# A planned attention and MLP kernel: the plan's charge for transposing DMAs, 0.8 to 0.67 and 0.5

## The chip, the cores and the metric

The kernel runs on one core of a Trainium2 chip, in one launch. The metric is the device time in microseconds (us) of that launch; of several runs the median is given. One execution more is taken with the hardware profiler. Its page and its trace count from the first to the last instruction, the span, and its own time is somewhat longer than its span.

The engines are TensorE (PE: matrix products; PEld: its weight loads), VectorE (DVE), ScalarE (ACT), GpSimd (POOL) and SyncE (SP). SyncE issues nearly all transfers; they run on 16 DMA engines that all transfers share.

## What is computed

A gated linear attention with a state per head, and behind it an MLP with a squared ReLU. The reference, cut to the arithmetic:

```python
# batch B=4, heads H=8, sequence S=768, head size D=48
for t in range(S):
    state = alpha[:, :, t, :, None] * state + np.einsum('bhd,bhe->bhde', k[:, :, t], v[:, :, t])
    y[:, :, t] = np.einsum('bhd,bhde->bhe', q[:, :, t], state)
x = y.transpose(0, 2, 1, 3).reshape(B * S, H * D)      # 3072 tokens x 384
h = x @ w_in                                           # 384 x 2048
r = np.maximum(h, 0.0)
out = (r * r) @ w_out                                  # 2048 x 384
```

Inputs and the output are float32; the products on TensorE are in bfloat16 with float32 sums.

## The kernel before

**Tiles.** The 3072 tokens are 24 chunks of 128, six to a batch entry. The attention works chunk by chunk: logarithms of alpha on ScalarE (L497), their running sums by a matmul with a triangle of ones (L530 to L546), exponentials of the sums (A, and their inverse) on ScalarE, and products of q with A and of k with the inverse on VectorE. Scores of a chunk are then a product of k and q (`e_p2`, L452), masked on VectorE (`sm`, L463, L472 and L473); the output is scores times v (L707) plus q times the state (L701). The state is updated by a matmul of k's product and v (L679), scaled on VectorE (L690), and copied to bfloat16 on ScalarE (L695).

Chunks 10 to 23 go in pairs (`DUO` = 10, `RAW` = 10): q and k are turned by a transposing DMA *before* they meet the exponentials. A q pair is loaded at L413, cast on GpSimd (L417) and turned by one transposing DMA (L420, tile rawt); k is loaded at L402, cast (L514) and a pair is turned by another (L517, tile aiT). VectorE multiplies the turned tiles with the exponentials (L610 for q, L613 for k). From chunk 18 on (`KTURN`) the k product is turned back by a transposing DMA for the state update (`e_kn`, L615). The casts of v (L506) are on GpSimd too.

The attention output is copied by ScalarE to `xn` (L487) and has to be turned once more, to be the MLP's moving operand `xT_big`. For chunks 14 to 22 (`XTURN`) a transposing DMA does it (`e_xt`, L729), for the others TensorE (L726) and a copy on VectorE (L489).

The MLP takes the chunks in groups, of two for the most part. Its first product with `w_in` goes to PSUM; ScalarE writes the ReLU `r` (L789), VectorE squares it into `gT` (L797); the second product takes `gT` and `w_out`; a copy on ScalarE or VectorE (L869, L871) moves the result out, and SyncE, or GpSimd for some, stores it. The first 16 chunks' outputs are held back (`keep`) and stored late, from L876.

**What sets the order.** No loop sets it. Each step is added to a plan as an operation with an engine, a duration in us, the operations that it depends on, and a latency. The plan then simulates the engines: at each step it starts the operation that can start first, and at equal times the one with the lower `prio`. In the end it sorts all operations by planned start and emits them in that order; each engine's queue gets its instructions in the order of emission and works them off in that order. A planned duration sets an order, then, and no time.

Loads are operations of a first-in-first-out engine called DMA (0.98 to 1.0 for 192 KB, 1.6 for a q pair). Transposing DMAs are of an engine called TR; each also keeps the engine DMA for its duration, in `Plan.run`, so that loads planned behind it start later:

```python
            if eng in ("OUT", "TR"):
                free["DMA"] = max(free.get("DMA", 0.0), t) + op.dur
            op.done = t + op.dur + op.lat
```

`TLD` is the charge for half a turned q or k pair (L420 and L517 are charged `2 * TLD`) and for the turned k product (L615 is charged `TLD`). `e_xt` has a charge of its own. `TLAT` and `XLAT` are the latencies behind the charges, `TLATE` and `late` put the instruction itself later in SyncE's queue than its planned start, so that loads can go ahead of it. A square of 128x512 on VectorE (L797) is charged 0.06 + 512/1850 = 0.34, a product of L610 or L613 0.34.

Which attention steps may run early is bounded by a gate: a chunk's sums may be added only when the MLP has come far enough. The instruction streams are the outcome of all of these together.

## Time and profile before

| what | before |
|---|---|
| median of 3 runs | 181.31 us (180.39 to 181.83) |
| the profiled execution | 181.09 us |
| its span | 179.4 us |
| granted TensorE clock, mean | 0.998 |
| HBM read, written | 25.17 MB, 4.72 MB |
| transposing DMAs xT, rawt, L615, aiT | 9, 7, 5, 7 |

The runs spread over 1.44 us, 0.8% of their median. The profiled execution is one run: its terms are added against its own 181.09, which is 1.7 above its span and 0.22 below the median.

Of a row in a timeline the first two numbers are start and length, then come engine, line, operation, what is written and read, and how many instructions were merged; square brackets tell of idle time before it. Rows of a DMA queue ("SPq") show the issue, not the transfer. Matmuls overlap each other: for two that follow each other the distance of their starts tells what one costs.

### The profile page before, as it was taken

To read this page: it belongs to the slowest core of one execution; us is meant where nothing else is said; L and a number is where in the kernel's file an instruction comes from. 1 tells how busy PE (TensorE), PEld (TensorE's weight loads), DVE (VectorE), ACT (ScalarE), POOL (GpSimd) and SP (SyncE) were. 2 spreads that over 40 slices of the span, in tenths; PEclk is the share of its full clock that TensorE was granted. 3 is DMA by queue.
4 is the path that set the end of the run, shared out by engine and by line. 5 is a ranking of instruction groups with operands and counts; after the bars stand their busy time and mean duration, and the time that the engine had idled before them with its cause. 6 is when DMAs were issued, how large, how long until landed. Compare 5 with 4: busy or idle time off the path is not lost.

```text
span 179.4 us, 4829 instructions
## 1 busy us (share of the span) xinstructions
PE 173.2 (97%) x1883; PEld 129.2 (72%) x1883; DVE 121.9 (68%) x264; ACT 124.2 (69%) x282; POOL 35.7 (20%) x76
## 2 busy tenths in 40 slices
PE   7899999899999999999999999999999999999993
PEld 2577884567869887779668766778967866888672
DVE  1279898784999995887977788368766675355100
ACT  3677799316859988889669964788974953679221
POOL 8221100011131171512506141023114211000000
PEclk9999999999999999999999999999999999999999
DMA  5999999999999999989999997797999852696112
GB/s 172 218 214 255 312 359 321 317 234 215 205 205 192 214 171 219 219 163 222 165 207 220 159 200 121 153 212 139 191 207 129 179 117 77 204 365 246 43 50 88
DMA packets 118487, 35.42 MB, mean 197 GB/s; under 512 B 110048, under 2 KB 117600, under 8 KB 118464
## 3 DMA queue, kind: packets, MB, share of 16 engines
q1 hardware_dynamic: 118336, 34.71, 87.2%
q8 instruction: 15, 0.25, 0.6%
q0 software_dynamic: 128, 0.39, 0.6%
q14 instruction: 8, 0.07, 0.1%
HBM read 25.17 MB, written 4.72 MB: 167 GB/s over the span
## 4 chain that ended last, share of the span: by engine, by line
PE 68%; ACT 13%; DMA 8%; DVE 7%; issue 2%; SPq 0%; ACTq 0%
PE bank L252 61%; DMA wi<-in_moe_w_in_dram 5%; ACT r L789 5%; DVE gT L797 3%; PE bank L255 3%; DMA at<-in_alpha_dram 2%; PE sc L252 2%; ACT qkT L550 2%; PE st L252 1%; DVE sm L463 1%; ACT aiT L554 1%; ACT Ainv L566 1%; ACT keep L871 1%; ACT L_s L497 1%; DVE qkT L613 1%
## 5 line engine op out<-in xcount | busy, mean ns | idle before, releaser
L252 PE MATMUL bank<-xT_big,w_in_b 128*128 128x256 bf16 (+2 forms) x636 | 73.8, 262 | 0.2
L252 PE MATMUL bank<-w_out_b,gT 128*128 128x384 bf16 (+1 forms) x400 | 70.7, 320 | 0.5 <-DVE w_out_b L308 0.5
L252 PEld LDWEIGHTS <-w_in_b 128*128 128x128 bf16 x636 | 53.8, 98 | 9.6 <-issue 0.8
L789 ACT ACTIVATE r<-bank 128x512 bf16<-128x512 f32 x96 | 55.8, 611 | 7.0 <-PE bank L252 5.6
L252 PEld LDWEIGHTS <-gT 128*128 128x128 bf16 x416 | 37.1, 98 | 19.4 <-DVE w_out_b L308 1.0
L797 DVE TENSOR_TENSOR gT<-r 128x512 bf16<-128x512 bf16 x96 | 41.4, 453 | 13.8 <-ACT r L789 12.0
L506 POOL CAST vb<-vt 128x384 bf16<-128x384 f32 x24 | 14.1, 588 | 71.8 <-DMA vt<-in_v_dram 59.2
L487 ACT CAST xn<-bank 128x384 bf16<-128x384 f32 x24 | 11.7, 488 | 13.9 <-PE bank L252 13.8
L690 DVE TENSOR_TENSOR st<-st,ae_s 128x384 f32<-128x384 f32 x20 | 11.2, 558 | 5.9 <-PE st L252 5.8
L252 PEld LDWEIGHTS <-qkT 64*128 64x128 bf16 (+1 forms) x272 | 10.5, 95 | 4.9 <-issue 2.8
L871 ACT COPY keep<-bank 128x384 f32<-128x384 f32 x13 | 6.2, 479 | 11.1 <-PE bank L252 11.0
L463 DVE TENSOR_TENSOR sm<-sc,utri_b 128x512 bf16<-128x512 f32 x20 | 12.8, 681 | 1.2 <-PE sc L252 1.1
L417 POOL CAST rawb<-q_s 128x384 bf16<-128x384 f32 x14 | 7.2, 540 | 29.4 <-DMA q_s<-in_q_dram 29.4
L463 DVE TENSOR_TENSOR sm<-bank,utri_q 128x512 bf16<-128x512 f32 x14 | 9.0, 684 | 4.6 <-PE bank L252 4.6
L252 PE MATMUL bank<-warm 128*128 128x256 bf16 (+1 forms) x54 | 9.9, 322 | 1.3 <-DVE warm L196 1.3
L695 ACT CAST sb<-st 128x384 bf16<-128x384 f32 x20 | 9.7, 486 | 1.9 <-DVE st L690 1.8
L603 DVE TENSOR_TENSOR qA_s<-q_s,A 128x384 bf16<-128x384 f32 x10 | 5.9, 588 | 7.5 <-ACT A L562 7.5
L497 ACT ACTIVATE L_s<-at 128x384 bf16<-128x384 f32 x20 | 10.4, 525 | 0.1
L610 DVE TENSOR_TENSOR qkT<-rawt,qkT 128x512 bf16<-128x512 bf16 x14 | 6.3, 465 | 4.6 <-ACT qkT L550 4.6
L550 ACT ACTIVATE qkT<-bank 128x512 bf16<-128x512 f32 x14 | 8.4, 602 | 1.1 <-PE bank L252 0.9
L606 DVE TENSOR_TENSOR kI_s<-kt,Ainv 128x384 bf16<-128x384 f32 x16 | 8.8, 553 | 0.5 <-ACT Ainv L566 0.5
L252 PE MATMUL bank<-vb,sm 128*128 128x48 bf16 x192 | 9.1, 183 | 0.0
(70 smaller groups left out, 174.5 us busy)
## 6 DMA issues: line engine op xcount, KB each, us to landing
kt<-in_k_dram SPq DMA_DIRECT2D x24, 192.0 KB, 4.5
vt<-in_v_dram SPq DMA_DIRECT2D x24, 192.0 KB, 4.0
at<-in_alpha_dram SPq DMA_DIRECT2D x20, 192.0 KB, 3.9
wo<-in_moe_w_out_dram SPq DMA_DIRECT2D x4, 768.0 KB, 8.9
out_dram<-keep SPq DMA_DIRECT2D x4, 768.0 KB, 6.2
q_s<-in_q_dram SPq DMA_DIRECT2D x7, 384.0 KB, 4.1
q_s<-in_q_dram SPq DMA_DIRECT2D x10, 192.0 KB, 4.7
wi<-in_moe_w_in_dram SPq DMA_DIRECT2D x4, 384.0 KB, 4.9
```

The source lines that it names most:

```text
L252: pin(nc.tensor.matmul(*a, **kw))
L463: pin(nc.vector.tensor_mul(d["sm"][:, hh], d["sc"][hh], mask.to_broadcast([P, NP, P])))
L487: pin(nc.scalar.copy(out_t, in_t))
L497: pin(nc.scalar.activation(L[:, :, 0:D], d["at"], AF.Ln))
L506: pin(nc.gpsimd.tensor_copy(d["vb"], d["vt"]))
L550: pin(nc.scalar.activation(d["qkT"][:, NP:2 * NP, :].rearrange("p n (r i) -> p n r i", r=2), d["pmT"].rearrange("p n (i r) -> p n r i", r= ...
L606: pin(nc.vector.tensor_mul(kI[:, :, 0:D], d["kt"], d["Ai"]))
L690: pin(nc.vector.tensor_mul(st4, st4, bcast(ae, D)))
L695: pin(nc.scalar.copy(d["sbt"], d["st"]))
L789: pin(nc.scalar.activation(o, x, AF.Relu))
L797: pin(nc.vector.tensor_mul(gT[g][:, f0:f0 + per, lo * P:lo * P + n], r, r))
L871: pin(nc.scalar.copy(box["ob"], box["po"]))
```

## The change

The charges of the transposing DMAs in the plan fall: `TLD` from 0.8 to 0.67 and that of `e_xt` from 0.8 to 0.5. Every other charge stays, those of loads and of VectorE's products among them; so do latencies, buffers, tiles and arithmetic.

```diff
@@ -326,7 +326,7 @@
-    TLD, TLAT, TLATE = 0.8, 5.0, 2.0
+    TLD, TLAT, TLATE = 0.67, 5.0, 2.0
@@ -727,7 +727,7 @@
             def e_xt():
                 pin(nc.sync.dma_start_transpose(out=xT_big[:, :, s % XR * P:(s % XR + 1) * P], in_=d["xn"]))
-            d["x"] = add("TR", 0.8, e_xt, xn, lat=XLAT)
+            d["x"] = add("TR", 0.5, e_xt, xn, lat=XLAT)
             d["x"].late = 1.8
             d["end"] = xn
             return
```

`TLD` is used in three places, all of them transposing DMAs:

```python
        d["qturn"] = add("TR", 2 * TLD, e_turn, *d["use_q"], ..., lat=TLAT)      # q pair, L420
                d["turn"] = add("TR", 2 * TLD, e_turn, C[s - 1]["kb"], d["kb"], ..., lat=TLAT)   # k pair, L517
                    d["mk"] = add("TR", TLD, e_kn, o, old, lat=KLAT)             # k product, L615
```

Both kernels issue the same matmuls, loads, transposes and stores. What differs is their order. GpSimd's is the same. SyncE's is the same up to the two k loads of chunks 18 and 19 (issued from 101.70 in the profile); behind these, loads of chunks 18 to 23 stand ahead of transposes that they followed. TensorE's, VectorE's and ScalarE's orders differ from the scores of chunks 10 and 11 on (73.71 in the profile). Of the copies of L869 and L871, one output copy goes from VectorE to ScalarE.

## The prediction

> **What bounds the kernel now.** I read the page first, its busy shares and the chain of work that ended last. Times are us from the span's start.

> ```profile
> PE 173.2 (97%) x1883; PEld 129.2 (72%) x1883; DVE 121.9 (68%) x264; ACT 124.2 (69%) x282; POOL 35.7 (20%) x76
> ...
> PE 68%; ACT 13%; DMA 8%; DVE 7%; issue 2%; SPq 0%; ACTq 0%
> ```

> TensorE is busy nearly throughout. A busy share can hide gaps, so next come the stretches of 20 us (columns: stretch, length, then busy time per engine, clock, DMA share, GB/s) and the chain in order of time.

> ```profile
> 60.00:80.00 20.00, 19.90 (x237) 16.15 (x236) 17.02 (x39) 17.12 (x39) 7.67 (x13) 1.00 1.02 202
> 80.00:100.00 20.00, 19.68 (x200) 15.37 (x198) 16.08 (x35) 16.68 (x42) 7.24 (x12) 1.00 1.12 201
> 100.00:120.00 20.00, 19.94 (x216) 13.70 (x216) 12.76 (x27) 14.32 (x38) 2.97 (x7) 1.00 0.88 167
> 120.00:140.00 20.00, 20.00 (x218) 15.74 (x215) 14.56 (x31) 15.18 (x34) 4.96 (x10) 1.00 0.99 169
> 140.00:160.00 20.00, 20.00 (x205) 15.24 (x204) 11.95 (x26) 12.40 (x27) 2.25 (x4) 1.00 0.63 176
> ```
> ```profile
> 119.08 0.04 issue
> 119.12 1.15 PE bank L252 x14
> ...
> 157.29 19.04 PE bank L252 x154
> 176.36 0.32 ACT ob L829
> ```

> From 119.12 to 176.36 the chain is TensorE alone: it never waits there. What waits are left after 60 lie between 75 and 120. Their size is read from starts in TensorE's timeline, since ends are modelled:

> ```profile
> 91.45 0.81 PE L252 MATMUL bank<-w_out_b,gT 128*128 128x384 bf16 x4
> 92.53 0.32 PE L252 MATMUL bank<-L_s,utri_b 128*128 128x384 bf16 x1 [0.27 <-ACT xn L487]
> ```

> Back to back, 128x384 matmuls start 0.162 apart (x8 in 1.46), so after four the next was due at 92.10 and came 0.43 late. The same count gives 0.26 at 75.52, about 0.24 between 89.97 and 91.17, 0.21 at 99.73 and 0.23 at 119.12: 1.4 us in all. That is the most that any reordering behind 72 can win, 0.8% of the time.

> **The change, part by part.** No instruction is added or removed but for how copies are shared (three keeps stay on VectorE; one output copy goes to ScalarE). Two charges in the plan fall: 0.80 to 0.67 for half a q or k transpose and for a k-product one (L615), 0.8 to 0.5 for an xT one. Instruction order decides the rest.

> *Is the charge right?* In a quiet stretch, 147.1 to 149.9, one L615 transpose runs with a store that has its own queue:

> ```profile
> q1 hardware_dynamic: 544, 0.13, 24.3%
> ```

> 24.3% of 2.8 is 0.68 us: the new 0.67. In the crowded stretch 58.3 to 101.1 (four pairs of chunks) the queue reads:

> ```profile
> q1 hardware_dynamic: 37691, 8.36, 103.1%
> ```

> 1.031 x 42.8 / 4 = 11.0 us of engine time per pair: one q pair, six loads, two transposes. With the plan's 1.6 and 6 x 1.0, a transpose there costs (11.0 - 7.6) / 2 = 1.7; by SyncE's clock it is (10.7 - 7.6) / 2 = 1.55, against 1.6 charged before and 1.34 now:

> ```profile
> 58.26 0.58 SPq L413 DMA_DIRECT2D q_s<-in_q_dram  x1
> ...
> 68.78 0.51 SPq L413 DMA_DIRECT2D q_s<-in_q_dram  x1
> ...
> 101.08 0.57 SPq L413 DMA_DIRECT2D q_s<-in_q_dram  x1
> 101.70 1.80 SPq L402 DMA_DIRECT2D kt<-in_k_dram  x2
> 103.55 1.43 SPq L402 DMA_DIRECT2D vt<-in_v_dram  x1
> 106.57 1.19 SPq L729 DMA_TRANSPOSE xT_big<-xn  x1
> ```

> (101.08 - 58.26) / 4 = 10.7. So the plan now expects each pair 0.4 us too early while the engines are full, 1.7 us after four pairs.

> *SyncE's and POOL's queues.* POOL's order is unchanged, SyncE's too up to the two kt loads at 101.70. To there nothing can arrive earlier: the engines set the pace. Behind it the xT transpose of chunk 14 goes ahead of the vt load of 103.55; in the trace SyncE then stood idle from 104.98 to 106.57 for xn, and now xn comes 3.7 us sooner on TensorE, so that idle time goes. Loads of chunks 19 to 23 pass xT, q/k and L615 transposes. Summing engine time in the new order from kt's landing at 107.02, at 1.07 a load, 1.58 a q pair, 1.5 a q or k transpose, 0.8 for L615, 0.6 for xT: k transposes of pairs 18, 20, 22 land by 115.5, 128.3, 141.1, where the trace has 115.25, 131.29, 145.63. Their scores move by +0.7, -1.95 and -2.6 us in TensorE's queue, so they keep or gain margin. Cost 0; the cover is that margin. L615 transposes have less: that of chunk 19 sums to 124.2 and its state matmul, 1.85 earlier, would stand at 125.1. Margin 0.9 (2.0 on average in the trace).

> *TensorE's order.* The same matmuls, 163.4 us of start-to-start work either way: cost 0 unless a step comes before its data. Shifts, counted in matmuls of the new order: scores (L452) of pair 10 by -0.33, 12 by -0.65, 14 by -3.64, 16 by -1.1. For a pair what counts is the way from the last cumulative-sum matmul (L546) over exp on ScalarE and the products on VectorE (L610, L613) to the scores. The quickest in the trace is 2.8 us (96.84 to 99.64). The new order leaves 3.9, 5.2, 4.0, 3.7, 3.8, 3.6, 3.9 for pairs 10 to 22: all above 2.8, the trace's own smallest being 3.5.

> *VectorE.* The products count as they did (0.34 start to start). What the count lacks shows at pair 12:

> ```profile
> 85.07 1.36 DVE L613 TENSOR_TENSOR qkT<-aiT 128x512 bf16<-128x512 bf16 x2
> 86.35 2.37 DVE L797 TENSOR_TENSOR gT<-r 128x512 bf16<-128x512 bf16 x5
> 88.64 1.28 DVE L463 TENSOR_TENSOR sm<-bank,utri_q 128x512 bf16<-128x512 f32 x2
> ```

> 0.64 apart while POOL's five casts run (84.31 to 87.44), against 0.34 later; masks L463 keep 0.6. Pair 12: scores come 0.65 earlier, one square (0.34 to 0.64) leaves the masks' way and the chain's first products can start up to 0.5 earlier: the wait of 0.67 there changes by -0.5 to +0.3; I take +0.1, nearest to the square alone. Pair 14: masks have 0.27 to spare ahead of L701, behind one product of 0.42: 0 to +0.4; I take 0. Pairs 16 and 20: casts may meet three products, 3 x 0.3 = 0.9, against margins of 0.9 and 0.8: 0 to +0.3 each; I take 0.1 together. Pair 10: masks wait for the same squares as before: 0 to +0.1, taken 0.

> [...]

> *Waits that may go.* Those at 99.73 and 119.12 (ScalarE's r, 0.44) sit among moved blocks: -0.44 to 0, taken -0.2, as half the blocks around them move.

> **Sum.** 0.1 + 0.1 - 0.2 = 0 on the profiled execution's 181.09 (span 179.4 and 1.7 around it). That run lies 0.2 under the median of 181.31; I forecast between them, **181.2**. All low ends with the other waits: -1.4, 179.7; all high ends: +0.1 + 0.3 + 0.4 + 0.6 = +1.4, 182.5.

> **Rivals.**
> *The loads don't gain anything* (in the stretch before 103.55 they can't, and TensorE needs none sooner): for it, the 103% above and a chain without DMA after 119. Time 181.1 to 181.3, the same as mine; it differs only in that landings stay where they were.
> *Slower: the queue behind the loads.* More loads stand ahead of the L615 transposes; state matmuls are in order, so each late one stops TensorE. Place: chunk 19 near 125. Margin 0.9; from 107.02 to there 17.2 us of transfers are summed, so a queue 16% slower than its crowded pace is 2.7 late and costs 1.8: 183.0. For it: the plan is 1.7 ahead of the engines there. Against it: pairs took 10.7 for 11.0 us of engine time, 3% less, not more. It decides above 5% (0.9 / 17.2).
> *Slower, smaller: masks late at pairs 12, 14 and 20* to the high ends: 182.5.
> *Faster:* all waits after 72 go, 179.7; against it, pair 12's masks stay behind VectorE's products.

> **How the numbers follow.** One per cent is 1.8 us, about what a measurement can tell here. My forecast, within its terms: 0.50. Loads without gain: 0.22. Late masks: 0.12, a third of it over 1%. Queue: 0.11, all over 1%. Faster rival: 0.05, mostly under 180. So slower 0.15, faster 0.04, same 0.81. The range takes in the late-mask end and the lower part of the queue's, and the spread of runs (180.39 to 181.83): 180.2 to 182.7.

> **What would show it.** Right: xT of chunk 14 issued near 103.6 with no idle time behind the kt loads; q loads of pairs 20 and 22 issued 3 us or more before 115.97 and 131.19; TensorE busy 19.9 or more in each stretch after 100; a tail like 157.29 to 176.36. Wrong: TensorE waiting for L615's transposes or for masks over 0.5 us at one place, or a landing of k's transpose of pair 20 behind 131.

## The result, and the profile after

| | before | after |
|---|---|---|
| median | 181.57 us (180.39 to 183.33, 6 runs) | 187.95 us (186.27 to 190.47, 6 runs) |
| ratio, with its 95% interval | | 1.034 (1.027 to 1.041) |
| the profiled execution | 181.09 us, span 179.4 | 188.31 us, span 186.6 |
| mean granted clock in it | 0.998 | 0.989 |

The forecast was 181.2 and no change. The kernel became 6.4 us slower. A median is of all runs; a ratio leaves out the few executions that were slower as a whole.

The page after, with the same two lines as before (busy time of each engine, then the chain of work that ended last):

```profile
PE 175.4 (94%) x1882; PEld 129.8 (70%) x1883; DVE 122.2 (65%) x263; ACT 125.0 (67%) x283; POOL 35.5 (19%) x76
...
PE 63%; DMA 12%; DVE 9%; ACT 7%; SPq 5%; issue 2%; DVEq 0%; ACTq 0%
```

TensorE's busy share falls from 97% to 94%, and DMA's part of the chain rises from 8% to 12%. The stretches of 20 us say where (columns: stretch, length, busy time of PE, PEld, DVE, ACT and POOL, clock, DMA share, GB/s):

```profile
80.00:100.00 20.00, 19.47 (x204) 14.73 (x202) 16.27 (x36) 15.90 (x39) 6.31 (x11) 1.00 1.05 192
100.00:120.00 20.00, 20.00 (x219) 14.53 (x219) 13.62 (x28) 15.05 (x37) 5.30 (x10) 1.00 1.05 175
120.00:140.00 20.00, 17.37 (x161) 12.84 (x158) 12.07 (x27) 14.15 (x34) 4.59 (x9) 0.91 0.90 179
140.00:160.00 20.00, 20.00 (x232) 15.95 (x232) 13.75 (x29) 13.68 (x30) 2.21 (x4) 1.00 0.57 116
```

Only 120 to 140 stands out: 2.63 us without TensorE's work, 161 matmuls against 218, and a clock of 0.91 where the three others have 1.00. TensorE's list of waits (total, times, longest) names the DMA, and the chain in order of time shows the place:

```profile
PE st L252 <- DMA kI_s<-qkT: 2.6, 1, 2.6
```
```profile
122.87 0.22 ACT r L789
123.09 5.08 DMA kI_s<-qkT
128.17 0.05 issue
128.22 0.50 PE st L252 x4
```

`kI_s<-qkT` is L615, the transposing DMA that turns a chunk's k product. That of chunk 18 is issued at 123.09 and lands 5.08 us later; the state matmul behind it starts at 128.22. Before, it was issued at 118.95, landed at 122.13, and the state matmul came at 124.89, with 2.75 us to spare.

This first profile of after holds one more loss, between 15 and 35 us, for the weights (`DMA wi<-in_moe_w_in_dram` is 9% of its chain). Below, "lost" is the distance of two matmul starts less 0.43 ns a column, about what back-to-back ones take in these traces (0.162 us for 128x384, 0.109 for 128x256, 0.055 for 128x128); a figure just below nothing means that nothing was lost. How much earlier a matmul stands in TensorE's order is counted by the same 0.43 ns, over the columns of the matmuls that are still to come. Lost between 15 and 40 are 4.3 us in this execution, and 1.9 in before. Four more profiles of after lost 2.1 to 2.2 there and took 186.46 to 188.14 us. So it is a draw of this one execution, and not the cause.

### The profile page after: what moved, and what is told of

It reads as the page before. It is cut to its first block, busy times and chain, and to the rows that moved or that the text cites. A ratio compares the mean times of both kernels' runs of the same rounds, so it can differ in the third digit from the quotient of the medians.

```text
span 186.6 us, 4834 instructions
## 1 busy us (share of the span) xinstructions
PE 175.4 (94%) x1882; PEld 129.8 (70%) x1883; DVE 122.2 (65%) x263; ACT 125.0 (67%) x283; POOL 35.5 (19%) x76
## 4 chain that ended last, share of the span: by engine, by line
PE 63%; DMA 12%; DVE 9%; ACT 7%; SPq 5%; issue 2%; DVEq 0%; ACTq 0%
PE bank L252 58%; DMA wi<-in_moe_w_in_dram 9%; SPq L402 5%; ACT r L789 3%; DVE sm L463 3%; DVE gT L797 3%; DMA kI_s<-qkT 3%; PE bank L255 2%; PE st L252 2%; PE sc L252 1%; ACT qkT L550 1%; DVE qkT L613 1%; ACT aiT L554 1%; DVE kI_s L606 1%; DVE w_in_b L308 1%
## 5 line engine op out<-in xcount | busy, mean ns | idle before, releaser
L252 PE MATMUL bank<-xT_big,w_in_b 128*128 128x256 bf16 (+2 forms) x635 | 75.6, 264 | 2.0 <-ACT w_in_b L310 1.8
L252 PE MATMUL bank<-w_out_b,gT 128*128 128x384 bf16 (+1 forms) x400 | 71.4, 321 | 0.5 <-DVE w_out_b L308 0.5
L252 PEld LDWEIGHTS <-w_in_b 128*128 128x128 bf16 x636 | 53.9, 98 | 12.3 <-ACT w_in_b L310 2.2
L797 DVE TENSOR_TENSOR gT<-r 128x512 bf16<-128x512 bf16 x96 | 41.5, 456 | 20.0 <-ACT r L789 19.0
L252 PEld LDWEIGHTS <-gT 128*128 128x128 bf16 x416 | 37.5, 98 | 19.7 <-DVE w_out_b L308 1.0
L506 POOL CAST vb<-vt 128x384 bf16<-128x384 f32 x24 | 13.4, 560 | 75.4 <-DMA vt<-in_v_dram 63.7
L487 ACT CAST xn<-bank 128x384 bf16<-128x384 f32 x24 | 11.6, 483 | 17.9 <-PE bank L252 17.8
L252 PEld LDWEIGHTS <-qkT 64*128 64x128 bf16 (+1 forms) x272 | 10.6, 95 | 4.8 <-issue 2.8
L463 DVE TENSOR_TENSOR sm<-sc,utri_b 128x512 bf16<-128x512 f32 x20 | 12.8, 681 | 1.0 <-PE sc L252 0.8
L252 PE MATMUL bank<-warm 128*128 128x256 bf16 (+1 forms) x54 | 10.1, 327 | 1.3 <-DVE warm L196 1.3
L871 ACT COPY keep<-bank 128x384 f32<-128x384 f32 x13 | 6.4, 491 | 6.7 <-PE bank L252 6.6
L463 DVE TENSOR_TENSOR sm<-bank,utri_q 128x512 bf16<-128x512 f32 x14 | 9.0, 680 | 2.7 <-PE bank L252 2.7
L606 DVE TENSOR_TENSOR kI_s<-kt,Ainv 128x384 bf16<-128x384 f32 x16 | 9.5, 594 | 1.3 <-ACT Ainv L566 1.1
L871 ACT COPY ob<-bank 128x384 f32<-128x384 f32 x7 | 3.3, 478 | 9.1 <-PE bank L252 9.1
L252 PE MATMUL st<-vb,kI_s 128*128 128x96 bf16 x80 | 6.8, 209 | 2.6 <-DMA kI_s<-qkT 2.6
(69 smaller groups left out, 179.4 us busy)
```

Of the source, the lines that this page charges most:

```text
L252: pin(nc.tensor.matmul(*a, **kw))
L463: pin(nc.vector.tensor_mul(d["sm"][:, hh], d["sc"][hh], mask.to_broadcast([P, NP, P])))
L487: pin(nc.scalar.copy(out_t, in_t))
L506: pin(nc.gpsimd.tensor_copy(d["vb"], d["vt"]))
L606: pin(nc.vector.tensor_mul(kI[:, :, 0:D], d["kt"], d["Ai"]))
L797: pin(nc.vector.tensor_mul(gT[g][:, f0:f0 + per, lo * P:lo * P + n], r, r))
```

## The experiments

**Theory A:** the plan now places chunks 18 to 20 earlier in TensorE's order, but SyncE's queue does not get there earlier, so TensorE waits for L615's transposes, and a slower clock may follow. **Rivals:** A1, the transfer is slow because loads issued right behind it share its engines; A2, something else holds one transfer up; D, the wait only moves to the next transposing DMA when it is mended; E, the time is lost elsewhere (the start, VectorE's masks).

### The two kernels again: e0_before and e1_after

> The kernel before, once more, for its profile. In the profile of the changed kernel TensorE loses about 3.7 us between 15 and 35 us, where before lost 1.7, though the order there is the same in both. If that comes from the draw of the run (weights landing late), this profile may lose 2 to 4 us there too; if it belongs to the changed kernel, this one loses 1.7 again, and its time is 181 to 182.

> The changed kernel once more. Theory A (TensorE waits for the L615 transpose of chunk 18): the wait of 2.6 to 2.8 us before the state matmul near 125 shows again, between 2 and 4 us, and a stretch of slower clock behind it; the time is 186.3 to 188.5. Rival B (the loss is in the start, between 15 and 35): the wait at the state matmul is under 1 us where the start loses less.

Measured: 181.73 and 186.46 us. In e1_after the wait is there again, 2.96 us at 126.32, with L615 issued at 120.90 and landing 5.37 later. What follows it is seen in shorter stretches of e1_after:

```profile
124.00:127.00 3.00, 0.68 (x13) 0.69 (x14) 0.54 (x2) 0.00 (x0) 0.33 (x2) 0.87 0.79 155
127.00:129.00 2.00, 2.00 (x14) 1.44 (x12) 1.50 (x4) 1.44 (x3) 0.33 (x1) 0.50 0.76 132
129.00:132.00 3.00, 3.00 (x35) 2.30 (x34) 1.01 (x3) 2.00 (x4) 0.51 (x1) 0.89 0.92 180
```

The clock column reads 0.50 from 127 to 129: TensorE runs at half speed behind the wait. Its 128x256 matmuls start 0.21 us apart there (nine in the 1.89 from 126.96), against 0.109 at a clock of 1.00. In steps of 0.2 us it is half from about 126.2 to 129.6, and from 128.0 to 131.4 in the first profile: 3.4 us each, worth half of that. TensorE lost 4.3 us between 120 and 145, against -0.3 in e0_before, and the times differ by 4.7. The start has nothing to do with it (2.2 lost from 15 to 40, e0_before 2.3). Theory A stands, E falls.

In e0_before the transpose of chunk 18 landed at 124.28 for a matmul at 124.50: a margin of 0.2, where the profile that the prediction was made from had 2.75. The margin differs by 2.5 us between executions of one kernel. A packet of program code explains most of it, as e4_phase shows below: in e0_before one starts at 122.11, while that transpose is under way, and it lands 4.94 us after its issue; in the other it starts at 122.21, just behind the landing, which took 3.19.

### Longer due times for L615: e2_klat

```diff
-    KLAT, KLATE = 5.0, 1.0
+    KLAT, KLATE = 8.5, 1.0
```

> The changed kernel with the plan's latency of the L615 transposes at 8.5 instead of 5.0 (KLAT), so that the state matmuls that need them stand some 3.5 us later in TensorE's queue; both new charges stay. Theory A: the wait at chunk 18 falls under 0.5 us, the slow clock behind it goes too, and the time falls by about 4 us, to 183 to 184.5. Rival B (start): no more than 1 us is won, 187. Rival C (masks and products late in the new order in general): no change beyond 1 us either, as their order up to chunk 18 is the same.

Measured: 187.1 us (184.47 to 187.99), ratio 1.022 (1.013 to 1.032). The wait at chunk 18 is gone, but the time does not fall as A expected. A wait of the same kind stands at the next late transposing DMA, one of xn, in TensorE's timeline:

```profile
146.10 0.50 PE L252 MATMUL bank<-xT_big,w_in_b 128*128 128x256 bf16 x3 [2.83 <-DMA xT_big<-xn]
```

The clock is 0.50 behind this one too, from about 146.5 to 149.9. That is D: mending one due time moves the wait.

### No load right behind L615: e3_hold

```diff
-... else LT, at=0.6)
+... else LT, at=119.0 if (s, nm) == (20, "vt") else 0.6)
```

> The changed kernel with the loads of v of chunk 20 and alpha of chunk 22 held back, so that they stand behind the L615 transpose of chunk 19 in the queue instead of between it and that of chunk 18. Theory A1 (the landing of a transposing DMA is stretched by loads queued right behind it: 5.1 us from issue to landing with them, 3.2 without): that of chunk 18 lands 3.2 to 3.6 us after its issue, the wait falls to 1.0 to 1.5 us, the time to 185 to 186.5. Rival A2 (it is late only because what stands ahead of it is late): it still takes about 5 us to land, wait and time as in the changed kernel.

Measured: 185.38 us (185.01 to 191.23), ratio 1.020 (1.015 to 1.025). L615 was issued at 122.16, the next load at 124.74; it still took 4.80 us to land, and the wait was 2.23. So A1 falls: the loads behind it are not what stretches the landing. The time does lie in the range that went with A1 (185 to 186.5), so it alone would have misled.

### Program code moved by 42 instructions: e4_phase, and its control e10_phase_before

In the first profiles a packet of queue q8, "instruction", with 16 KB, starts 2.6 us after the issue of chunk 18's L615 (at 125.67 and 123.47) and takes 1.4 to 1.8 us. It is one packet; that it holds up one of the 16 DMA engines is the author's reading. The DMA view of a later execution (e12_after_a, 135 to 141, 40 slices of 0.15 us) shows the transfers around such a packet:

```profile
DMA  6102438999999999999999990100009999999999
GB/s 132 36 8 56 74 49 177 237 256 259 248 256 259 247 250 256 280 369 205 67 9 13 6 6 2 9 9 10 9 14 243 262 262 177 238 227 230 222 215 261
...
q8 instruction: 1, 0.02, 1.2%
...
kI_s<-qkT SPq DMA_TRANSPOSE x2, 3.6
```

The packet starts at 137.56 and takes 1.18 us. From 138.0 to 139.5 the transfers move 2 to 14 GB/s, where it is some 250 before and behind. The digits of the first line give a packet's whole time to the slice in which it starts; they are 1 and 0 from 138.6, since hardly any packet starts there that takes long. In the packet records 29 packets that start between 137.76 and 138.56 all end at 139.5: all of them wait. That it is for the one engine with the code packet is not shown (the records don't name the engine). Chunk 20's L615 lands 4.78 us after its issue there. The packets of TensorE's code come every 10 to 16 us between 100 and 150. From one packet to the next TensorE has 249 instruction rows on average in before and 254 in after (146 to 326), in 11.5 and 11.8 us. That is near the 256 and the 11 to 12 us of the expectation below. TensorE itself they don't hold up in before, where it never waits behind 119.12, with packets at 122.21, 136.25 and 146.52. They do hold up the transposes that meet them (4.5 to 5.4 us to landing for 2.7 to 3.3, see below).

The edit issues the dummy matmuls at TensorE's start as half as many of twice the width, so that every later packet should come about 42 instructions later:

```diff
-                for _ in range(n):
-                    mm(wp[:, 0:256], lhsT=warm[:, 0:P], rhs=warm[:, 0:256], start=True, stop=True)
+                for x in range(0, n, 2):
+                    w = 256 * min(2, n - x)
+                    mm(wp[:, 0:w], lhsT=warm[:, 0:P], rhs=warm[:, 0:w], start=True, stop=True)
```

> The changed kernel, but TensorE's dummy matmuls at its start are issued as half as many of twice the width: the same work and the same busy time with 42 fewer instruction rows. Theory A2 (a 16 KB packet of program code for TensorE, one per 256 of its instructions or about 11 to 12 us, falls on the transfer of chunk 18's L615 transposes and makes one of the 16 DMA engines late): the packets all come about 42/256 of 11.5 us = 1.9 us later, at 125.4 to 127.6, when most of that transfer is done; issue to landing falls from 5.0 to 5.4 us to 3.3 to 4.2, TensorE's wait from 2.6 to 3.0 to 1.0 to 1.9, its granted clock stays above 0.97 between 120 and 140, and the time is 183.3 to 185.0. Rival A1 (the transfer is slow because of the loads that share the engines): landing still 4.8 to 5.4 after issue, the wait 2.6 or more with the lower clock, time 186.3 to 188.3.

> The kernel before, with the dummy matmuls at TensorE's start issued as half as many of twice the width, as in e4_phase: a control for that edit. Theory: the edit alone costs nothing, and moves the packets of program code about 1.9 us later, from 122.2 to about 124; with 0.2 to 2.8 us of margin on chunk 18's transposes the time stays at 181.2 to 182.6. Rival: the edit itself changes the time by over 1% (below 179.9 or above 183.6), and e4_phase then says nothing of the packets.

Measured: e4_phase 184.40 us (183.46 to 185.03), ratio 1.013 (1.009 to 1.018). The packet came at 127.60, chunk 18's L615 landed 2.88 us after its issue, and TensorE's timeline has these state matmuls of chunks 18, 19 and 20:

```profile
123.65 0.35 PE L252 MATMUL st<-vb,kI_s 128*128 128x96 bf16 x4 [0.23 <-DMA kI_s<-qkT]
...
126.78 0.34 PE L252 MATMUL st<-vb,kI_s 128*128 128x96 bf16 x4 [0.64 <-DMA kI_s<-qkT]
...
138.92 0.34 PE L252 MATMUL st<-vb,kI_s 128*128 128x96 bf16 x4 [1.67 <-DMA kI_s<-qkT]
```

The clock stayed at 1.00. The control is unchanged by the edit: 181.29 us, ratio 0.998 (0.994 to 1.001), with its packet at 124.34 instead of 122.21. So A2 holds, and the 17 profiles (all but e5_k18's) bear it out: chunk 18's L615 landed 4.5 to 5.4 us after its issue in the ten where such a packet started 2 us or more before the landing, and 2.7 to 3.3 us after it in the other seven. A packet that meets the transpose is worth about 2 us of landing. With none on those of chunks 18 to 20 the kernel is 2.7 us over before (184.40 less 181.74) instead of 6.4, each in its own series of runs. These 2.7 us agree with the 2.54 us of waits in the rows above.

### More of chunk 18: e5_k18 and e11_k18_again

```diff
-                    d["mk"] = add("TR", TLD, e_kn, o, old, lat=KLAT)
+                    d["mk"] = add("TR", TLD, e_kn, o, old, lat=8.5 if s == 18 else KLAT)
```

> The changed kernel, but the plan is told that chunk 18's L615 transpose alone takes 3.5 us longer to land, so that it puts that one state matmul later in TensorE's order; charges and the other due times stay. Theory A (that one wait, with the lower clock behind it, is the 5 to 6 us): no wait above 1 us before a state matmul, clock above 0.97 between 120 and 140, time 181.7 to 183.5. Rival D (the whole tail of the plan is too early, so the next transposing DMA is late instead): a wait of 2 us or more for another transposing DMA after 126 us, time 185 to 188. Rival E (the time is lost elsewhere): the wait goes and the time stays at 186 or more without another wait.

> e5_k18 once more, since its profiled execution was stretched to 615 us on every engine and shows nothing. Theory A: chunk 18's wait is gone; what is left are waits of under 1.5 us at the next transposing DMAs, time 182 to 184. Rival D (the next one waits in its place, with a wait of 2.5 us or more and the clock at half behind it): 185 to 188.

The profiled execution of e5_k18 took 615.92 us: TensorE alone was slow in it (128x384 matmuls start 0.63 apart throughout, for 0.162; VectorE's 124 and GpSimd's 33 us of work are about as ever), and so it shows nothing of the waits. Why it was slow is not known. The profiled one of e11_k18_again took 183.41, as A expected, with no wait of TensorE's for a transposing DMA behind 120. But of the other six runs of this kernel only one is like it (183.77); five took 186.56 to 189.85, with mean clocks of 0.979 to 0.991. None of these was profiled, so what they wait for is not known. Inconclusive.

### Each charge alone: e6_tld_only, e7_xt_only

Each is the changed kernel with the other charge set back:

```diff
-            d["x"] = add("TR", 0.5, e_xt, xn, lat=XLAT)
+            d["x"] = add("TR", 0.8, e_xt, xn, lat=XLAT)
```
```diff
-    TLD, TLAT, TLATE = 0.67, 5.0, 2.0
+    TLD, TLAT, TLATE = 0.8, 5.0, 2.0
```

> Only the turns and L615 are charged less (0.67 for 0.8), the transposes of xn are charged 0.8 as before. By theory A the plan runs ahead of SyncE by a part of what both charges do (0.26 + 0.26 us a pair of chunks for the turns, 0.26 for L615 from chunk 18 on, against 0.6 for xn): the state matmul of chunk 18 stands about 1 us earlier than before and its transposes land 0 to 1.5 us later; wait 0 to 2.3 us, no lower clock, time 182 to 184.5. Rival (either charge alone is enough to put some transposing DMA behind TensorE by over 2.8 us): 186 to 188.

> Only the transposes of xn are charged less (0.5 for 0.8), turns and L615 0.8 as before. Theory A: about half of the lead that the two charges give together, so the wait for chunk 18's L615 is 0 to 2.3 us, no lower clock, time 182 to 184.5; it should be the smaller share, since SyncE spends 1.2 us on issuing a transpose whether it is charged 0.5 or 0.8, and only two are issued a pair. Rival (either charge alone is enough): 186 to 188.

Measured: 185.23 us (183.22 to 186.34), ratio 1.016 (1.009 to 1.022), with `TLD` alone; 182.95 (182.72 to 183.54), ratio 1.007 (1.005 to 1.010), with xT's charge alone. The first lies above what A expected: its profile has a wait of 2.34 us at chunk 18 and the half clock behind it. The second is as expected, with waits of 0.35 and 0.96 at chunks 18 and 20. The smaller step in the number (0.13) does more harm. It counts twice for a q or k pair, and for L615 as well: alone it puts chunk 18's state matmul 2.0 us and chunk 20's 3.5 us earlier than before, xT's charge alone 0 and 2.5.

### Due times for both, and the charge the other way: e8_kx, e9_xt12

e8_kx is the changed kernel with `KLAT` 8.5 for 5.0 and `XLAT` 10.5 for 7.0. e9_xt12 is the kernel before with one charge raised:

```diff
-            d["x"] = add("TR", 0.8, e_xt, xn, lat=XLAT)
+            d["x"] = add("TR", 1.2, e_xt, xn, lat=XLAT)
```

> The changed kernel, but the plan is told that the L615 transposes land 3.5 us later (8.5 for 5.0) and the transposes of xn 3.5 us later (10.5 for 7.0): the charges of the change stay, the due times allow for the queue as it runs. Theory A (the waits for transposing DMAs, and the lower clock behind those of 2.5 us and more, are the whole loss): no such wait above 1 us, clock above 0.99 over 120 to 160, time 181.3 to 183.0. Rival D (the plan's tail is still too early, so that some other step waits, turns or loads): 184 or more with a wait of 2 us elsewhere. Rival E (the loss lies elsewhere): waits gone and 185 to 188.

> The kernel before, with the charge of xn's transposes moved the other way: 1.2 us, what SyncE spends on issuing one, for 0.8; turns and L615 0.8. Theory A (what paces the queue is SyncE's issue time and the full queue behind it, so that a higher charge puts TensorE's due steps later and the transposes nearer to their due times): no wait above 0.7 us for a transposing DMA, time 181.0 to 182.5. Rival G (any other order than the one before meets some late transfer, whichever way the charges go): a wait of 1.5 us or more and 183 to 186.

Measured: e8_kx 183.82 us (183.34 to 185.71), ratio 1.013 (1.005 to 1.021): it is 1.8 over before on its chip (182.00), where after was 6.4 over, with no single wait over 1.03 for a transposing DMA and the clock at 1.00 to 152, in a profile of its slowest execution. It is 0.8 above what A expected, since small waits remain in several places (L615 1.3 us in two, ScalarE's r 0.68, VectorE's product 0.48). e9_xt12 is 181.90 (181.53 to 183.62), ratio 1.002 (0.998 to 1.005), with no wait of TensorE's for a transposing DMA at all. Chunk 20's state matmul stands 2.9 us later there than in before. A different order by itself did no harm, then; those that were ahead of the queue did. SyncE's issue of an xT transpose takes 1.2 us at the least in all these timelines, which is the figure tried here. Neither this kernel nor e10_phase_before, which both leave before's charges or raise one, is measurably faster than before.

### Three more profiles of after, and the wait filled: e12_after_a to e14_after_c, e15_warm18

Several timed runs of after have a mean clock of 1.00 and are as slow, while the two profiled so far had 0.989.

> The changed kernel, a third profiled execution. Its timed runs lie between 186.3 and 190.5 us, some with a mean granted clock of 0.99 and some of 1.00, and only two with 0.989 have been profiled. Theory A: a wait for chunk 18's L615 transposes of over 2 us in every execution; where the clock is 1.00 the wait is under 2.5 us at chunk 18 and further waits for transposing DMAs, 1 to 2.5 us together, follow at chunks 19 to 22 or at xn's transposes. Rival B (the loss at the start, for the weights, that the first profile shows between 15 and 35 us): 2 us or more of TensorE's idle time before 40 us, and less behind 120.

> The changed kernel, a fourth profiled execution; as for e12_after_a.

> The changed kernel, a fifth profiled execution; as for e12_after_a.

Measured: 188.12, 188.14 and 187.52 us. A wait of over 2 us at chunk 18 was expected of every execution, and only the first of the three has it. TensorE's state matmuls of chunks 18, 19 and 20 in e12_after_a, then in e14_after_c:

```profile
125.49 0.34 PE L252 MATMUL st<-vb,kI_s 128*128 128x96 bf16 x4 [2.05 <-DMA kI_s<-qkT]
127.83 0.33 PE L252 MATMUL st<-vb,kI_s 128*128 128x96 bf16 x4
140.34 0.34 PE L252 MATMUL st<-vb,kI_s 128*128 128x96 bf16 x4 [2.05 <-DMA kI_s<-qkT]
```
```profile
124.45 0.34 PE L252 MATMUL st<-vb,kI_s 128*128 128x96 bf16 x4 [0.60 <-POOL rawb L514]
128.76 0.34 PE L252 MATMUL st<-vb,kI_s 128*128 128x96 bf16 x4 [1.80 <-DMA kI_s<-qkT]
141.55 0.34 PE L252 MATMUL st<-vb,kI_s 128*128 128x96 bf16 x4 [2.32 <-DMA kI_s<-qkT]
```

In brackets stands the idle time before each. (In e14_after_c the 0.60 is put down to GpSimd; L615 landed at 124.41, 0.04 before the matmul, so it was the DMA.) The five profiles side by side:

| profile of after | us from L615's issue to its landing, chunks 18, 19, 20 | TensorE's idle time there | half clock | lost from 120 to 145 |
|---|---|---|---|---|
| first | 5.08, 4.38, 3.15 | 2.63, 0, 0 | behind chunk 18 | 3.9 |
| e1_after | 5.37, 4.66, 3.11 | 2.96, 0, 0 | behind chunk 18 | 4.3 |
| e12_after_a | 4.97, 4.28, 4.78 | 2.05, 0, 2.05 | behind chunk 20 | 5.7 |
| e13_after_b | 3.06, 4.10, 4.95 | 0.40, 1.10, 2.52 | none | 4.1 |
| e14_after_c | 3.02, 4.76, 4.46 | 0.60, 1.80, 2.32 | none | 4.8 |

Before lost -0.4 and -0.3 there in its two profiles. So the place changes with the run, and the sum much less: 3.9 to 5.7 us until TensorE is back in step with the queue. Where one wait is long, or the clock falls behind it, the next transposes are in time. Both profiles at clock 1.00 lose their time at the same three matmuls.

e15_warm18 puts nine matmuls of zeros in front of chunk 18's state matmul, which starts the state afresh:

```diff
                 st = d["st"] = state["ps"]
+                for _ in range(9 if s == 18 else 0):
+                    mm(st.rearrange("p n e -> p (n e)"), lhsT=warm[:, 0:P], rhs=warm[:, 0:NP * 2 * D],
+                       start=True, stop=True, skip_group_check=True)
```

> The changed kernel with nine matmuls of zeros, 128x384, into the state's tile ahead of chunk 18's state matmul, which clears it; they fill 1.4 us of its wait with work that nothing needs. Theory (the half clock behind the wait comes from TensorE's standing still for 2.5 us or more, and is worth 1.3 to 1.5 us): the state matmul starts as late as before, 2.4 to 3.1 us behind its turn, TensorE's idle time there is 1.0 to 1.7 us, the granted clock stays at 1.00 in every 20 us of the profile, and the time is 184.0 to 186.0. Rival (the half clock has another cause, such as the transfers or the power of the chip): 0.85 to 0.92 between 120 and 140 all the same, and 187 to 189.

Measured: 186.99 us (186.68 to 188.35), ratio 1.029 (1.018 to 1.040), 1 us above the range. Idle time at chunk 18 was 0.80, and the clock from 120 to 160 was 1.00 in its profile; but 1.97 us of waiting stood at chunk 20. That is much the same sum once more (1.5 filled, 0.80 and 1.97 idle). Since e13_after_b and e14_after_c keep the full clock without the filling, this run alone does not show what brings the half clock; the last section compares all profiles.

## Why the prediction was wrong, point by point

*What bounds the kernel* was read rightly: TensorE. No order that was tried took it measurably below before.

*The charge.* The text found that a q or k transpose costs 1.55 to 1.7 us in the crowded queue, against 1.6 charged before and 1.34 now, and that the plan would be early by 0.4 us a pair. Right in sign, and too small. Behind the state matmuls of chunks 18, 19 and 20 stand 51.9, 49.8 and 36.4 us of matmuls in before, and 54.0, 51.7 and 41.1 in after: their turns come 2.1, 1.9 and 4.7 us earlier. (The prediction's 1.85 for chunk 19 was right.)

*SyncE's queue and its margin* are the step that failed: "Cost 0; the cover is that margin", and "Margin 0.9" for L615. Loads were to go forward in time: q loads of pairs 20 and 22 3 us before 115.97 and 131.19, and k transposes to land by 128.3 and 141.1. In the five profiles of after these q loads came at 115.6 to 118.2 and at 129.7 to 132.4, and the k transposes landed at 131.2 to 134.0 and at 144.6 to 148.0. SyncE's rows of before, then those of after, from chunk 18's q load to chunk 20's L615:

```profile
101.08 0.57 SPq L413 DMA_DIRECT2D q_s<-in_q_dram  x1
...
118.95 2.50 SPq L615 DMA_TRANSPOSE kI_s<-qkT  x2
...
134.06 3.63 SPq L615 DMA_TRANSPOSE kI_s<-qkT  x2
```
```profile
105.39 0.57 SPq L413 DMA_DIRECT2D q_s<-in_q_dram  x1
...
123.09 1.21 SPq L615 DMA_TRANSPOSE kI_s<-qkT  x1
...
125.65 2.58 SPq L615 DMA_TRANSPOSE kI_s<-qkT  x1
...
138.65 1.59 SPq L615 DMA_TRANSPOSE kI_s<-qkT  x1
```

To chunk 20's L615 it is 33.0 us before and 33.3 after (32.7 and 32.9 in e12_after_a and e1_after), with one load more ahead of it (30 transfers for 29). A lower charge made the plan's queue faster and the real one not at all.

At chunk 20 before had next to nothing to give. Its state matmul follows a landing at 138.79:

```profile
140.02 0.33 PE L252 MATMUL st<-vb,kI_s 128*128 128x96 bf16 x4
```

That is 1.23 us to spare, and in e0_before and e10_phase_before, which have the same order, it is 0.11 and 0.05. With its turn 4.7 us earlier and its transpose no earlier, TensorE had to lose some 3.4 to 4.6 us by then, an estimate from these figures; lost from 120 to 145 are 3.9 to 5.7. (A code packet met chunk 20's transpose in all three of these profiles of before's order. In e4_phase none did, and there the waits come to 2.54.)

*The sum over engine time* was not what failed. From the kt load's landing to that of chunk 19's L615 it gave 17.2 us. The five profiles of after took 18.6 to 18.9, 9% more, but in all of them a code packet met that transpose; in e4_phase, where none did, it was 17.3. (For the k transposes of pairs 18, 20 and 22 the sum is 3 to 6% short there.) Its start was off: kt lands at 107.02 in the one execution that the prediction was made from, at 108.70 in e0_before, and at 108.5 to 111.2 in the five profiles of after.

*The margin* was wrong for four reasons. It was taken from one execution, and e0_before had 0.2 us at chunk 18 where that one had 2.75. It was worked out at chunk 19 alone, while chunk 18's turn came 2.1 us earlier and chunk 20's 4.7. The "2.0 on average" hid the 1.23 of chunk 20. And the code packets, about 2 us on a landing that they meet, were not thought of.

*The rival that came true* is "the queue behind the loads": the sign was right, and so was the place, near 125. Its reason, a queue 16% slower than its crowded pace, was not: without packets the queue kept within 6% of the sum, and the turns went ahead of it. So its price of 1.8 us (183.0), near the 2.7 of e4_phase, is in part luck. It lacked chunk 20, the packets and the half clock: 188 instead of 183. Its chance, 0.11, rested on pairs having taken 3% less than their engine time in the crowded stretch. That stretch had no L615 transposes in it, and a share of 103.1% of 16 engines shows that the recorded times of packets overlap, so the 11.0 us a pair are no measure of the pace.

*VectorE, masks and waits that may go* stayed within the range that was summed for them: lost from 60 to 120 are 0.1 to 1.3 us in the five profiles of after, and 0.4 and -0.6 in the two of before. That is some 0.8 us more on average; which of these terms it is, is not shown. Late masks are not where the 6.4 us went.

*The signs named ahead* decided it: TensorE waits for L615 over 0.5 us at one place, and k's transpose of pair 20 lands behind 131 in all five profiles, as it did in before (131.29): the loads' new places gained it nothing.

## What to carry to other kernels

A charge in a plan is right when the plan's queue keeps the pace of the real one, not when it equals the engine time of a lone transfer: compare the plan's clock with the issue times of the queue over a long stretch before lowering one. When a reordering brings a consumer forward, count for every later consumer of that queue how far its turn moves against the landing, and take the margin from several executions. A margin under about 2.5 us on a transposing DMA was not one here: at chunk 18 before had 2.75 us in one execution and 0.2 in another.
